# Two chains of memory segments rebuilt: output sums of all heads in three column groups of PSUM, padded memory keys, sums of exponentials redone backward

## The chip, the cores and the metric

The kernel runs on one core of a Trainium2 chip. The metric is the device time of one execution in microseconds (us), lower is better. A quoted time is the median of several executions; repeats of one kernel lie within about 0.3%. On one core a run counts as slow only if it is more than 1.5% above the fastest of the same kernel.

Engines in the profile lines: PE is TensorE's matmuls, PEld its weight loads, DVE VectorE, ACT ScalarE, POOL GpSimd, SP SyncE.

## The reference, cut to what matters

The program computes a gated mix of a plain attention A and a recurrent memory attention B, forward and with all gradients. Only B matters here. Its 2048 tokens are 64 segments of 32; each segment carries 8 rows of memory of width 576, and 32 heads of width 128 attend over memory and tokens together:

```python
for s in range(n_seg):                       # 64 segments, one after another
    h = concat([mem, x[s*32:(s+1)*32]])      # 8 + 32 rows of 576
    q, k, v = h @ Wq, h @ Wk, h @ Wv         # 32 heads of 128
    p = softmax(where(mask, q @ k.T * 128**-0.5, -1e9))   # memory keys are seen by all rows
    o = (p @ v) @ Wo
    mem = o[:8]                              # the next segment needs this
    outs.append(o[8:])
```

The kernel computes the memory rows of all segments first (the forward chain), then all token rows at once (the token attention), then the gradient of the memory from the last segment to the first (the backward chain), then the token gradients, the memory rows in token order, and the weight gradients. The two chains are serial: a segment can't start before the one ahead of it has given its memory or its gradient.

## The kernel before: the parts that matter

The forward chain, one segment, cut:

```python
for wi, w in enumerate("qkv"):               # 8 memory rows times a weight, four column groups of 512
    ... 40 matmuls into two banks of 32 x 512 blocks, evacuation to qkv
    for g in range(4):
        nc.gpsimd.dma_start(self.MT[w][...], qkv[32 * g:32 * g + MEM])   # rows for later stages
    ... 8 transposes, compacted: mE[:, wi, :] holds head by head 8 columns
for r in range(2):                           # memory keys: 16 heads against 16 heads, mask keeps the diagonal
    self.mm(S[:, 256 + r * P:...], lhsT=mE[:, 1, cs], rhs=mE[:, 0, cs], ...)
nc.scalar.activation(ET[:, :], S[:, :], ACT.Exp, scale=SCALEB)
... transposes of memory values, copy to vc, sums, value matmuls
nc.vector.reciprocal(rl[:, :, 0], po[:, 2, 0:2])
nc.gpsimd.dma_start(self.RL_m[s]..., rl[:, :, 0])            # reciprocals kept for backward
for ri in range(8):                          # output projection: head g of each four in column group g
    for lo, hi in ((0, 512), (512, D)):
        for g in range(4):
            self.mm(pw[32 * g:32 * g + 32, lo:hi], lhsT=oT[:, c0:c0 + 32], rhs=WoN[:, h, lo:hi], ..., tp=(0, 32 * g))
nc.vector.tensor_copy(ws[:, 0:320], pw[:, 0:320])            # fp32
nc.scalar.copy(ws[:, 320:D], pw[:, 320:D])
for kt in range(NKT):                        # fp32 matmuls add the four groups and turn rows to columns
    self.mm(pm[:, kt, :], lhsT=ws[:, kt * P:(kt + 1) * P], rhs=self.selF[:, :])
nc.vector.tensor_copy(mT[:, :, (s + 1) * MEM:(s + 2) * MEM], pm[:, :, :])
```

The backward chain has the same shape: 40 matmuls give dO from the gradient of the memory, a multiplication by the stored reciprocals follows, then transposes, dP, dS, three projections with the transposed weights (one pass each over 32 heads), and the same fp32 reduction. Exponentials, reciprocals and outputs come back from DRAM. In the token attention the rows of memory keys and values come from DRAM, four DMA loads each:

```python
def load_mt(self, sp, name, src, tt, r):
    ... # the tile t
    for g in range(4):
        self.nc.gpsimd.dma_start(t[32 * g:32 * g + 32, :], src[tt * 32:(tt + 1) * 32, ...])
```

The softmax here doesn't subtract the row's maximum and nothing guards it: scores larger than these inputs give would overflow.

Of the kernel before, what the change touches and what calls it, by code (L numbers as in the profile page):

```python
# [29 lines left out]
class Kern:  # L30
# [41 lines left out]

    def setup_consts(self, pool):
# [8 lines left out]
        nc.gpsimd.memset(self.onesB[:], 1.0)  # L82
        self.negonesB = pool.tile([P, P], BF16, name="negonesB")
# [10 lines left out]
        mc = pool.tile([P, 512], BF16, name="maskC")  # L94
        nc.gpsimd.memset(mc[:], 0.0)
        for ri in range(8):
            for g in range(4):
                c0 = ri * 32 + g * 8
                keep_block(mc[:, c0:c0 + 8], 8, 32 * g, 32 * g + 32)
        for r in range(2):  # L100
            for ig in range(16):
                c0 = 256 + r * 128 + ig * 8
                keep_block(mc[:, c0:c0 + 8], 8, 8 * ig, 8 * ig + 8)
        self.maskC = mc
# [26 lines left out]
        sel = pool.tile([P, MEM], F32, name="selF")  # L131
        nc.gpsimd.memset(sel[:], 0.0)
        for g in range(4):
            nc.gpsimd.affine_select(out=sel[:], in_=sel[:], compare_op=ALU.not_equal, fill=1.0, base=-32 * g,
                                    pattern=[[-1, MEM]], channel_multiplier=1)
        self.selF = sel
# [7 lines left out]
    def setup_dram(self, dram):  # L144
        T, NSEG, NM, NTT = self.T, self.NSEG, self.NM, self.NTT
        DT = lambda shape, name, dt=BF16: dram.tile(shape, dt, name=name)
        self.xT_dram = DT([NKT, P, T], "xT_dram")
        self.a_dram = DT([T, D], "a_dram")
        self.db_dram = DT([T, D], "db_dram")

        self.XT = {w: DT([T, J], f"xt_{w}") for w in "qkv"}
        self.XE = {w: DT([NTT, P, J], f"xe_{w}") for w in "qkv"}

        self.MT = {w: DT([NM, J], f"mt_{w}") for w in "qkv"}

        self.XS = {w: DT([NSEG, P, 1024], f"xs_{w}") for w in "kv"}
        self.ME = DT([NSEG, P, 3, 256], "me")
        self.ET_m = DT([NSEG, P, 512], "et_m")
        self.OT_m = DT([NSEG, P, 256], "ot_m")
        self.RL_m = DT([NSEG, 2, P], "rl_m", F32)  # L160
        self.OX = DT([T, J], "ox")
        self.OM = DT([NM, J], "om")

    def load_B_fwd(self, pool):
        nc = self.nc
        self.Wq4 = pool.tile([P, 4, J], BF16, name="Wq4")
        self.Wk4 = pool.tile([P, 4, J], BF16, name="Wk4")
        self.Wv4 = pool.tile([P, 4, J], BF16, name="Wv4")
        self.Wqk5 = pool.tile([P, J], BF16, name="Wqk5")
        self.Wv5 = pool.tile([64, J], BF16, name="Wv5")  # L170
        for W4, Wd in ((self.Wq4, self.B_Wq), (self.Wk4, self.B_Wk), (self.Wv4, self.B_Wv)):
            for kt in range(4):
                nc.sync.dma_start(W4[:, kt, :], Wd[kt * P:(kt + 1) * P, :])
        nc.sync.dma_start(self.Wqk5[0:64, :], self.B_Wq[512:576, :])
        nc.sync.dma_start(self.Wqk5[64:128, :], self.B_Wk[512:576, :])
        nc.sync.dma_start(self.Wv5[0:64, :], self.B_Wv[512:576, :])
# [8 lines left out]
    def w_nat(self, w, kt):  # L185

        if kt < 4:
            return {'q': self.Wq4, 'k': self.Wk4, 'v': self.Wv4}[w][:, kt, :], slice(0, 128)
        if w == 'q':
            return self.Wqk5[0:64, :], slice(0, 64)  # L190
        if w == 'k':
            return self.Wqk5[64:128, :], slice(64, 128)
        return self.Wv5[0:64, :], slice(0, 64)

    def b_project(self, keep, sp, psum):
# [6 lines left out]
        for tt in range(NTT):  # L202
            tok = slice(tt * P, (tt + 1) * P)
            for w in "kvq":
                tk = sp.tile([P, J], BF16, name="p_tok", bufs=2)
                te = sp.tile([P, 2, 4, 4, P], BF16, name="p_em", bufs=2)
                for c in range(8):
                    pb = psum.tile([P, 512], F32, name="p_pb", bufs=4)
                    for kt in range(NKT):
                        wap, rows = self.w_nat(w, kt)  # L210
                        self.mm(pb[:, :], lhsT=xT[rows, kt, tok], rhs=wap[:, c * 512:(c + 1) * 512],
                                start=(kt == 0), stop=(kt == NKT - 1))
# [14 lines left out]
    def b_chain_fwd(self, keep, sp, psum, WoN):  # L227
# [11 lines left out]
        self.mT = mT  # L239
        for s in range(NSEG):  # L240
            tt, sl = s // 4, s % 4
# [6 lines left out]
            mE = sp.tile([P, 3, 256], BF16, name="c_mE", bufs=2)  # L248
            S = psum.tile([P, 512], F32, name="c_S", bufs=1)
            self.mm(S[:, :], lhsT=self.identB[:, :], rhs=self.maskC[:, :], start=True, stop=False)  # L250
            for wi, w in enumerate("qkv"):
                qkv = sp.tile([P, 2, 512], BF16, name="c_qkv", bufs=4)
                for r in range(2):
                    pb = psum.tile([P, 512], F32, name="c_pb", bufs=2)
                    for kt in range(NKT):
                        wap, rows = self.w_nat(w, kt)
                        for g in range(4):
                            c = 4 * r + g
                            self.mm(pb[32 * g:32 * g + 32, :], lhsT=mT[rows, kt, s * MEM:s * MEM + 32],
                                    rhs=wap[:, c * 512:(c + 1) * 512], start=(kt == 0), stop=(kt == NKT - 1),  # L260
                                    tp=(rows.start, 32 * g))
                    self.evac(qkv[:, r, :], pb[:, :])
                for g in range(4):
                    nc.gpsimd.dma_start(self.MT[w][s * MEM:(s + 1) * MEM, :].rearrange("t (r g n) -> g t r n", r=2, g=4)[g],
                                        qkv[32 * g:32 * g + MEM, :, :])
                pt = psum.tile([P, 8, 4, 32], BF16, name="c_tr", bufs=1)
                for ri in range(8):
                    self.tr(pt[:, ri].rearrange("p g m -> p (g m)"), qkv[:, ri // 4, (ri % 4) * E:(ri % 4 + 1) * E], P)
                self.evac(mE[:, wi, :].rearrange("p (a g m) -> p a g m", a=8, g=4), pt[:, :, :, 0:MEM])
            nc.gpsimd.dma_start(self.ME[s], mE[:, :, :])  # L270
            for ri in range(8):
                self.mm(S[:, ri * 32:ri * 32 + 32], lhsT=kx[:, ri, :], rhs=mE[:, 0, ri * 32:ri * 32 + 32],
                        start=False, stop=False)
            for r in range(2):
                cs = slice(r * P, (r + 1) * P)
                self.mm(S[:, 256 + r * P:256 + (r + 1) * P], lhsT=mE[:, 1, cs], rhs=mE[:, 0, cs], start=False, stop=(r == 1))
            ET = sp.tile([P, 512], BF16, name="c_ET", bufs=2)
            nc.scalar.activation(ET[:, :], S[:, :], ACT.Exp, scale=SCALEB)
            nc.gpsimd.dma_start(self.ET_m[s], ET[:, :])
            pv = psum.tile([P, 2, P], BF16, name="c_tr", bufs=1)  # L280
            for r in range(2):
                self.tr(pv[:, r, :], mE[:, 2, r * P:(r + 1) * P], P)
            vc = sp.tile([P, 2, P], BF16, name="c_vc", bufs=2)
            self.evac(vc[:], pv[:], use="v")
            po = psum.tile([P, 3, P], F32, name="c_o", bufs=1)
            for r in range(2):
                xs, ms = slice(r * P, (r + 1) * P), slice(256 + r * P, 256 + (r + 1) * P)
                self.mm(po[:, 2, r:r + 1], lhsT=ET[:, xs], rhs=self.onesB[:, :], start=True, stop=False)
                self.mm(po[:, 2, r:r + 1], lhsT=ET[:, ms], rhs=self.onesB[:, :], start=False, stop=True)
            for r in range(2):  # L290
                self.mm(po[:, r, :], lhsT=ET[:, 256 + r * P:256 + (r + 1) * P], rhs=vc[:, r, :], start=True, stop=False)
                for i in range(4):
                    c0 = r * P + i * 32
                    self.mm(po[32 * i:32 * i + 32, r, :], lhsT=ET[:, c0:c0 + 32], rhs=vx[:, r, i * E:(i + 1) * E],
                            start=False, stop=True, tp=(0, 32 * i))
# [4 lines left out]
            with nc.allow_non_contiguous_dma(reason="column of reciprocals"):  # L300
                nc.gpsimd.dma_start(self.RL_m[s].rearrange("r p -> p r"), rl[:, :, 0])
            for i in range(4):
                nc.gpsimd.dma_start(
                    self.OM[s * MEM:(s + 1) * MEM, :].rearrange("m (r g i e) -> i g m r e", r=2, g=4, i=4)[i],
                    oc[32 * i:32 * i + 32, :, :])
            pt = psum.tile([P, 2, P], BF16, name="c_tr", bufs=1)
            for r in range(2):
                self.tr(pt[:, r, :], oc[:, r, :], P)
            oT = sp.tile([P, 280], BF16, name="c_oT", bufs=2)
            nc.gpsimd.memset(oT[:, 256:280], 0.0)  # L310
            nc.vector.tensor_copy(oT[:, 0:256], pt[:].rearrange("p r n -> p (r n)"))
            nc.gpsimd.dma_start(self.OT_m[s], oT[:, 0:256])
            if s == NSEG - 1:
                break
            pw = psum.tile([P, 640], F32, name="c_pw", bufs=1)
            for ri in range(8):
                for lo, hi in ((0, 512), (512, D)):
                    for g in range(4):
                        h = (ri // 4) * 16 + g * 4 + ri % 4
                        c0 = ri * 32 + g * MEM  # L320
                        self.mm(pw[32 * g:32 * g + 32, lo:hi], lhsT=oT[:, c0:c0 + 32], rhs=WoN[:, h, lo:hi],
                                start=(ri == 0), stop=(ri == 7), tp=(0, 32 * g))
            ws = sp.tile([P, 640], F32, name="c_ws", bufs=1)
            nc.vector.tensor_copy(ws[:, 0:320], pw[:, 0:320])
            nc.scalar.copy(ws[:, 320:D], pw[:, 320:D])
# [1082 lines left out]
```

## Time and profile before

11818.32 us median of four runs (11794.58 to 11826.19); the profiled execution spans 11807.0 us. I cut the run at the first and last starts of each stage's tiles; clock is the mean that the throttle granted TensorE in the stage, 1.00 being full speed.

| stage | us | clock |
|---|---|---|
| attention A, projections, weights | 5937 | |
| forward chain | 1420 | 0.81 |
| token attention | 1511 | 0.77 |
| backward chain | 1151 | 0.88 |
| token gradients | 983 | 0.74 |
| memory rows | 118 | 0.51 |
| weight gradients | 687 | |

How to read it: a chain's stage is 63 spacings between segments plus a start, so the spacing of the copies that write the memory is its best measure (22.14 us forward, 17.07 backward, means). The lines of the stages, of a forward segment and of the waits are in the prediction (in the timeline: start, length, engine, line, what, count, in brackets the idle time before it).

### The profile page before, as it was taken

Reading aid. Unit: us, or ns where it says so; the run is one execution under the profiler, and the core shown is the slowest. Engines: PE = TensorE matmul, PEld = TensorE weight load, DVE = VectorE, ACT = ScalarE, POOL = GpSimd, SP = SyncE. Lnnn points to the kernel's source line nnn. Section 1 sums busy time; section 2 is a strip of 40 time slices with the busy share of each in tenths; the row PEclk is TensorE's granted clock in tenths of the full one; section 3 lists DMA queues with packets and bytes.
Section 4 is the critical chain, followed back from the end, with each engine's and each line's share of the span. In section 5 each row is a group of like instructions: output and inputs, shape, how many; then the busy total and the mean of one; then the engine's idle time right before and its main releaser. Section 6 shows DMA issues by size and latency. Waiting matters only on the chain. (4 is left out here: it accounts for less than half of the span.)

```text
span 11807.0 us, 189310 instructions
## 1 busy us (share of the span) xinstructions
PE 10704.6 (91%) x79411; PEld 4101.3 (35%) x79798; DVE 4365.5 (37%) x6102; ACT 3510.0 (30%) x4681; POOL 2793.4 (24%) x5477
## 2 busy tenths in 40 slices
PE   7999999999999999989888888888887888999799
PEld 2212121212121212134433333555544554555444
DVE  4555555555555555534311111333332222122200
ACT  3444444444444444423311111222221111111100
POOL 3000000000000000013245555333334444333100
PEclk8555555555555555589888877777778988777799
DMA  2000000000000000045532222555544333555544
GB/s 66 1 4 1 4 1 4 1 4 1 4 1 1 4 1 1 1 144 231 201 83 54 54 55 70 190 174 167 176 152 149 90 93 94 186 188 187 192 147 145
DMA packets 583499, 980.07 MB, mean 83 GB/s; under 512 B 213801, under 2 KB 392114, under 8 KB 564402
## 3 DMA queue, kind: packets, MB, share of 16 engines
q1 hardware_dynamic: 421506, 632.91, 16.9%
q0 software_dynamic: 159824, 333.70, 8.4%
q8 instruction: 624, 10.22, 0.4%
q14 instruction: 233, 1.91, 0.1%
q10 hardware_dynamic: 1312, 1.33, 0.0%
HBM read 542.17 MB, written 425.07 MB: 82 GB/s over the span
## 5 line engine op out<-in xcount | busy, mean ns | idle before, releaser
L1178 DVE TENSOR_TENSOR a_U<-a_w,a_E 128x1024 bf16<-128x1024 f32 x1024 | 1252.1, 1224 | 1131.5 <-ACT a_E L1176 1088.1
L1105 DVE TENSOR_TENSOR a_U<-a_w,a_E 128x1024 bf16<-128x1024 f32 x1024 | 1253.4, 1225 | 962.5 <-ACT a_E L1103 962.3
L1176 ACT ACTIVATE a_E<-a_w 128x1024 bf16<-128x1024 f32 x1024 | 1049.1, 1025 | 1375.6 <-PE a_w L66 1373.1
L1103 ACT ACTIVATE a_E<-a_w 128x1024 bf16<-128x1024 f32 x1024 | 1048.8, 1025 | 1179.5 <-PE a_w L66 1179.5
L66 PE MATMUL a_w<-a_kaug,a_qaug 19*128 19x512 bf16 x2048 | 901.7, 600 | 4.8 <-ACT a_E L1176 4.1
L66 PE MATMUL a_w<-a_vaugT,a_doaT 19*128 19x512 bf16 x2048 | 836.0, 620 | 22.0 <-DVE a_U L1178 16.1
L66 PE MATMUL a_acc<-a_E,a_dog 128*32 128x512 bf16 x2048 | 625.0, 600 | 71.8 <-ACT a_E L1176 0.2
L66 PE MATMUL a_w<-a_doT,a_vaugT 19*128 19x512 bf16 x2048 | 670.8, 623 | 5.2 <-ACT a_E L1103 4.0
L66 PE MATMUL a_w<-a_qaug,a_kaug 19*128 19x512 bf16 x2048 | 658.0, 599 | 3.6 <-ACT a_doT L63 3.0
L1137 POOL TENSOR_TENSOR a_otok<-a_tk,a_rl 128x144 bf16<-128x144 f32 x64 | 27.4, 428 | 2570.8 <-DVE a_rl L1136 2570.8
L66 PE MATMUL a_acc<-a_U,a_ku 128*32 128x512 bf16 x2048 | 625.3, 607 | 0.2
L66 PE MATMUL a_acc<-a_U,a_qtok 128*32 128x512 bf16 x2048 | 623.1, 606 | 0.6 <-DVE a_U L1178 0.6
L66 PE MATMUL w_acc<-w_col,w_h 128*128 128x512 bf16 (+1 forms) x2352 | 523.4, 381 | 13.5 <-DMA w_col<-dqx 10.8
L1081 POOL DMA_DIRECT2D a_dog<-do_dram x8 | 4.7, 589 | 1814.1 <-PE a_acc L66 1810.0
L61 DVE CAST p_tok<-p_pb 128x512 bf16<-128x512 f32 x384 | 265.4, 692 | 318.4 <-PE p_pb L66 318.4
L66 PEld LDWEIGHTS <-a_qaug 19*128 19x128 bf16 x2048 | 152.2, 98 | 655.5 <-issue 655.5
L66 PE MATMUL a_acc<-a_E,a_evB 128*64 128x512 bf16 x1024 | 325.6, 612 | 54.0 <-ACT a_E L1103 0.6
L66 PEld LDWEIGHTS <-w_h 128*128 128x128 bf16 (+1 forms) x2400 | 237.4, 100 | 299.6 <-issue 34.3
L66 PEld LDWEIGHTS <-a_dog 128*32 128x32 bf16 x2048 | 108.9, 100 | 652.4 <-issue 652.2
L63 ACT COPY p_em<-p_tr 128x512 bf16<-128x512 bf16 x384 | 225.0, 586 | 357.8 <-PE p_tr L71 357.6
L66 PEld LDWEIGHTS <-d_g 128*32 128x32 bf16 x12288 | 271.4, 104 | 170.8 <-issue 60.7
L66 PEld LDWEIGHTS <-a_ku 128*32 128x32 bf16 x2048 | 105.9, 101 | 639.3 <-issue 639.2
(476 smaller groups left out, 16390.7 us busy)
## 6 DMA issues: line engine op xcount, KB each, us to landing
xt_k<-p_tok SPq DMA_DIRECT2D x16, 1024.0 KB
xe_k<-p_em POOLq DMA_DIRECT2D x16, 1024.0 KB
xs_k<-p_seg POOLq DMA_DIRECT2D x64, 256.0 KB
xt_v<-p_tok SPq DMA_DIRECT2D x16, 1024.0 KB
xe_v<-p_em POOLq DMA_DIRECT2D x16, 1024.0 KB
xs_v<-p_seg POOLq DMA_DIRECT2D x64, 256.0 KB
xt_q<-p_tok SPq DMA_DIRECT2D x16, 1024.0 KB
xe_q<-p_em POOLq DMA_DIRECT2D x16, 1024.0 KB
```

Source lines behind the costliest of these rows:

```text
L61: nc.vector.tensor_copy(out, in_)
L63: nc.scalar.copy(out, in_)
L66: return self.nc.tensor.matmul(out, lhsT, rhs, start=start, stop=stop, tile_position=tp, skip_group_check=True)
L1081: nc.gpsimd.dma_start(dog[:, :, :], self.do_dram[g])
L1103: nc.scalar.activation(ex[:], s[:], ACT.Exp, scale=SCALEA)
L1105: nc.vector.tensor_tensor(out=u[:], in0=d[:], in1=ex[:], op=ALU.mult)
L1137: nc.gpsimd.tensor_tensor(out=osl, in0=v[:, :, :, o0:o0 + DA], in1=rl[:].to_broadcast([P, 4, 2, DA]), op=ALU.mult)
L1176: nc.scalar.activation(ex[:], s[:], ACT.Exp, scale=SCALEA)
L1178: nc.vector.tensor_tensor(out=u[:], in0=d[:], in1=ex[:], op=ALU.mult)
```

## The change

It shortens the path of a segment. The output sums of all heads collect in PSUM itself: each head's 576 columns are cut into three groups of 192 that run side by side, and all 32 heads accumulate, so that a bf16 copy of 96 rows and seven small bf16 matmuls replace the fp32 reduction. Memory keys and values stay padded, which saves the transposes of the values. The sums of exponentials over memory keys, and their reciprocals, are no longer stored but redone in the backward chain; rows that went to DRAM in token order are made by transposes where they are needed, or in the stage of the memory rows. "Filler" matmuls on a spare bank are to hold the clock through short waits. The diff, cut to its core:

```diff
+    def busy(self, pf, n, rhs):
+        w = rhs.shape[-1]
+        for _ in range(n):
+            self.mm(pf[0:32, 0:w], lhsT=self.identB[:, 0:32], rhs=rhs)
 # forward chain
-                for g in range(4):
-                    nc.gpsimd.dma_start(self.MT[w]..., qkv[32 * g:32 * g + MEM, :, :])
+            self.busy(pf, 2, mE[:, 0:512])            # after the scores
+            self.busy(pf, 4, ET[:, :])                # after the value matmuls
+            self.busy(pf, 4, oc[...])                 # after the transposes of the output
-                for lo, hi in ((0, 512), (512, D)):
-                    for g in range(4):
-                        self.mm(pw[32 * g:32 * g + 32, lo:hi], lhsT=oT[...], rhs=WoN[:, h, lo:hi], ...)
+                for g in range(4):
+                    for j in range(3):
+                        self.mm(pw[32 * j:32 * j + 32, :], lhsT=mEw(3, c0, c0 + 32), rhs=Wo[:, h, 192 * j:192 * j + 192],
+                                start=(ri + g == 0), stop=(ri + g == 10), tp=(0, 32 * j))
 # ... cut ...
+    def rows_to_columns(self, sp, psum, pre, pw, dst, late):
+        nc.scalar.copy(ws[0:96, 128:192], pw[0:96, 128:192])
+        nc.vector.tensor_copy(ws[0:96, 0:128], pw[0:96, 0:128])
+        self.busy(self.pf, 2, late)
+        for kt, p0, j, c0, n in (...):                # 3 matmuls that need the first copy, 4 that need the second
+            self.mm(pt[p0:p0 + n, kt, :], lhsT=ws[0:96, c0:c0 + n], rhs=self.identB[0:96, 32 * j:32 * j + 32], tp=(0, p0))
+        self.busy(self.pf, 1, late)
+        nc.vector.tensor_copy(dst, pt[:, :, 0:MEM])
 # backward chain
+            self.mm(S[:, :], lhsT=self.identB[:, :], rhs=self.maskD[...], start=True, stop=False)   # scores redone
+            ...
+            nc.scalar.activation(ET[:, 256:512], S[:, :], ACT.Exp, scale=SCALEB)
+            for x in range(2):
+                self.mm(Sg[:, 1, :], lhsT=self.onesPB[:, :], rhs=ET[:, 256 * x:256 * x + 256], ...)
+            nc.vector.reciprocal(rlb[:, :], Sg[:, 1, :])
-                nc.vector.tensor_tensor(out=dO[:, r], in0=pb[:], in1=rl[:, r].to_broadcast([P, 4, E]), op=ALU.mult)
+                self.evac(dO[:, r], pb[:, :], use="vs"[r])
+            self.busy(self.pf, 2, dO[:, 0])
+            self.busy(self.pf, 1, dO[:, 1])
 # ... 8 transposes of dO, product with rlb ...
+            self.busy(self.pf, 3, dO[:, 1])
+            self.busy(self.pf, 2, dOc[...])           # after dP
 # token attention (token gradients alike)
-                mv = self.load_mt(sp, "x_mv", self.MT["v"], tt, r)
+                mv = self.tok_me(sp, psum, "x_mv", me, 1)          # four transposes and a copy
 # the token gradients load the transposed weights again, after the backward chain
```

The count per backward segment: eleven fillers (3 and 3 of 512 columns around dO, 2 of 256 after dP, 3 of 512 in the reduction).

## The prediction

> **What bounds the kernel now.** The page's two lines of busy shares say that TensorE is busy nearly everywhere, but the granted clock differs from slice to slice, so I cut the run into stages (ends read from first and last starts of each stage's tiles) and asked for the table of stretches. Columns: stretch, its length in us, busy time and count of PE, weight loads, DVE, ACT, POOL, then granted TensorE clock, DMA share, GB/s.
>
> ```profile
> 5937.00:7361.00 1424.00, 1233.97 (x15740) 535.73 (x15741) 279.86 (x670) 217.23 (x479) 771.21 (x1340) 0.81 0.24 60
> 7361.00:8905.00 1544.00, 1273.87 (x11181) 761.56 (x11305) 507.02 (x1045) 431.12 (x772) 571.68 (x925) 0.77 0.53 177
> 8905.00:10022.00 1117.00, 954.54 (x18817) 566.86 (x18817) 279.09 (x672) 119.49 (x288) 516.17 (x1007) 0.89 0.33 96
> 10022.00:11002.00 980.00, 948.71 (x7101) 503.00 (x7199) 189.75 (x447) 161.87 (x288) 325.18 (x734) 0.74 0.58 184
> 11002.00:11115.00 113.00, 58.73 (x433) 45.00 (x432) 45.23 (x154) 30.04 (x57) 43.15 (x112) 0.52 0.90 279
> ```
>
> In order: forward chain, token attention, backward chain, token gradients, memory rows. The change leaves the first 5937 us and the last 692 us (weight gradients) as they are. The chains, 2541 us together, are 64 segments one after another: each needs the memory that the one before made. So no engine's share bounds them; the latency of one segment does. From the starts of the copy that writes a segment's memory I took the spacing: forward mean 22.13 us (20.2 to 24.1), backward mean 17.06 us (mostly 16.7 and 17.4 in turn).
>
> The timeline shows where a forward segment's time lies; these are the lines between its scores and the next segment (start, length, engine, line, what; in brackets idle time before it).
>
> ```profile
> 6617.79 0.60 ACT L278 ACTIVATE c_ET<-c_S 128x512 bf16<-128x512 f32 x1
> ...
> 6619.08 0.29 DVE L61 COPY c_vc<-c_tr 128x256 bf16<-128x256 bf16 x1 [0.51 <-PE c_tr L71]
> ...
> 6621.27 0.29 DVE L311 COPY c_oT<-c_tr 128x256 bf16<-128x256 bf16 x1 [0.45 <-PE c_tr L71]
> ...
> 6621.62 2.14 PE L66 MATMUL c_pw<-WoN,c_oT 128*32 128x512 bf16 x64 [0.45 <-DVE c_oT L311]
> ...
> 6623.89 0.49 DVE L324 COPY c_ws<-c_pw 128x320 f32<-128x320 f32 x1 [2.32 <-PE c_pw L66]
> 6624.41 0.37 ACT L325 COPY c_ws<-c_pw 128x256 f32<-128x256 f32 x1 [6.03 <-DVE c_ws L324]
> ...
> 6624.43 1.28 PE L66 MATMUL c_o<-selF,c_ws 128*128 128x8 f32 x10 [0.67 <-DVE c_ws L324]
> ...
> 6625.75 0.20 DVE L330 CAST c_mT<-c_o 128x40 bf16<-128x40 f32 x1 [1.37 <-PE c_o L66]
> 6626.01 1.05 PE L66 MATMUL c_pb<-Wq,c_mT 128*32 128x512 bf16 x16 [0.29 <-DVE c_mT L330]
> ...
> 6642.04 4.03 PE L66 MATMUL c_pw<-WoN,c_oT 128*32 128x512 bf16 x64 [0.45 <-DVE c_oT L311]
> ```
>
> The reader is to see two things. The reduction after the output projection (copies in fp32, DVE then ACT, ten fp32 matmuls, a copy) takes from 6623.76 to 6626.01, 2.25 us of hand-over. And the same 64 matmuls last 2.14 us in one segment and 4.03 us in the next: a segment with idle stretches pays the half clock later, on its dense matmuls. DMA is not the limit in either chain (shares 0.24 and 0.33).
>
> The waits of TensorE tell which stages have slack for added TensorE work:
>
> ```profile
> PE x_p L66 <- POOL x_pr L495: 102.8, 128, 1.7
> PE x_b L66 <- DMA g_mo<-om: 12.1, 1, 12.1
> ```
>
> The first is the longest in the token attention, the second in the token gradients, where it is a single start-up wait. So the gradients (PE busy 948.71 of 980) have no slack at all, the attention has some.
>
> **What the Trainium skill says.** "TensorE: Matmul & The Clock Gate", Part 1, has the array at half rate after idle windows of about 3.4 us and at full rate after a busy one; the 2.14 against 4.03 us agrees. Its Part 3 has matmuls in different 32-column groups run side by side; here 64 projection matmuls of 512 and 64 columns follow one another in 1.96 us (in the backward chain, from the first matmul with Wk at 9450.61 to the first with Wq at 9452.57), which is 32 x 576 columns / 4 groups / 2.4 columns per ns = 1.92 us, so it agrees. "PSUM — Partial Sum Buffer", PSUM bank collisions, wants accesses of two engines to one bank kept apart; the DVE and ACT halves of the fp32 copy above do run in turn. "TensorEngine Tiling (Array Packing)", Key Properties, says that a change of tiling mode drains the array; in the chains the 64-row matmul quads take 0.33 us and the 128-row ones 0.243 us, which fits. The change keeps those.
>
> **The change, part by part. Forward chain, one segment, at full clock.**
> - Projections q, k, v stay: six blocks of 0.97 + 0.33 = 1.30 us, with some twenty transposes between (four take 0.33 us): 7.8 + 1.65 = 9.45; the warm part of the trace runs slightly slower, so 9.7. Before, q ran at half clock in most segments (2.38 us a block, not 1.30).
> - From the last v matmul to the output projection: 6617.04 to 6621.62 = 4.6 us before. Memory values are now used from the padded rows, so the transposes and copy to c_vc (about 0.8 us between the end of the exponential and the first matmul that uses c_vc) go. New: 16 small score matmuls at about 0.026 us spacing (0.42, before 0.5), exponential 0.6, sums and 16 value matmuls 0.75, reciprocal 0.17, scaling 0.42, transposes 0.28, copy 0.29, eight hand-overs of about 0.07: 3.75 us. Filler matmuls (2, 4 and 4 of 512, 512 and 256 columns: 0.43, 0.85, 0.43 us) lie in waits of about that length.
> - Output projection: 32 heads, three groups of 192 columns side by side: 192/2.4 = 80 ns a head, 2.56 + 0.2 us latency. That uses three quarters of the groups: 0.6 us slower than 2.14, but far below 4.03.
> - Reduction: ACT copy of 64 columns 0.22, DVE 128 columns 0.28, in turn; seven bf16 matmuls 0.3; copy 0.2; hand-overs 0.3: 1.35 us for 2.25.
> - Sum: 9.7 + 3.75 + 2.75 + 1.35 = 17.5 us against 22.13. Times 63: **-290 us**. POOL's DMA issues (4 x 3 rows of q, k, v, four of om and others, over 10 us a segment) go as well; beside the path today, but they would not have fitted well in 17 us.
>
> **Backward chain, one segment.** dO matmuls 2.6 (same). Copy, transposes, product with the reciprocals (now on the transposed side, 0.42 for 0.29), dP: about 3.0 (2.74 before). From dP to the projection 1.1 (2.4 before), because dS is halved and v's heads start as soon as their gradient is there. Projection 96 heads x 82 ns = 7.85, with transposes and the q, k gradients between, 0.45, latency 0.15: 8.45 (6.7 before, partly at half clock). Reduction 1.35 (2.26). Redone scores, exponential, sums: 0.8 us of PE for segment s-1, mostly in waits, 0.2 on the path. Sum 16.7 against 17.06: **-23 us** over 63. What the reduction gives, the three-group projection takes. The weights come first for dO (4.7 MB, then 13.8 MB), so the first segment starts some 12 us sooner: **-12**.
>
> **What is paid elsewhere.**
> - Token gradients: a second load of the transposed weights, 13.8 MB, at the 420 GB/s that the stretch 8895 to 8915 shows is 33 us; a third may load early, and 12 us of start-up wait are there today: +22. Rows now made by transposes, 8 a half-tile at 0.08 to 0.15, and 16 matmuls with minus ones, 0.25 to 0.4: 1.15 us x 32 = +37, on a TensorE with no slack.
> - Token attention: the same 8 transposes, 0.65 to 1.2 us x 32 = 30, but with waits to hide in: +10.
> - Memory rows: 16 blocks for 12 at about 7 us: +28.
> Together **+97 us**.
>
> Total: -290 - 23 - 12 + 97 = -228; 11819.84 - 228 = about 11592, and I add 8 us for start-up of the new pools: 11600.
>
> **Rivals.** (1) The fillers do not hold the clock: dense matmuls then stay at 0.81 to 0.9 as now; about 1.5 us a forward segment and 0.7 a backward one come back (estimate: the excess of 4.03 over 2.14, and q's, in half the segments), total about 11730. For it: the clock follows activity in windows of some 3.4 us (same section), and fillers are only 0.2 to 0.85 us. Against it: they fill just the waits listed above. (2) Three groups of 192 run slower than 80 ns a head, because three weight loads a head are not hidden: at 100 ns the backward chain loses 1.9 us a segment, the forward 0.6: about 11755. Against it: weight loads of four groups start together in the trace. (3) A fixed instruction order makes the redone sums or fillers stall TensorE: +0.5 us a segment is +63 us. (4) The chain falls further, to 16.5 and 16, because more of the redone work and the fillers hide than I count: about 11480. (5) Memory traffic bounds a chain: shares of 0.24 and 0.33 speak against it.
>
> **Range and chances.** The gain I derive, 220 us, is 1.9%; the line of 2% lies at 11583, inside the uncertainty of the chains (some 40 us each) and of the costs elsewhere (25). So faster or same is nearly a coin toss, with a slight lean to same since sums of latencies leave things out; slower would need rivals 1 to 3 together. Range 11470 to 11720.
>
> **What would show it.** Spacing of the copies that write the memory: 17.5 forward, 16.7 backward. Granted clock near 1.0 in both chains. Output projection of 32 heads in about 2.75 us, in every segment alike; no fp32 matmul. Token gradients about 1040 us, memory rows about 140. Wrong if the clock stays under 0.9, if a head takes well over 80 ns, or if TensorE waits on a recomputed sum in the backward chain.

## More of the kernel before

In the timeline of the kernel before (start, length, engine, line, what, count, in brackets the idle time before it) the 40 dO matmuls stand in one piece of 2.68 us, the transposes of dS begin 6.13 us after the first of them:

```profile
9440.22 2.68 PE L66 MATMUL d_pb<-WoTb,d_gT 128*32 128x512 bf16 x40 [0.28 <-DVE d_gT L725]
...
9446.35 0.37 PE L71 MATMUL d_tr<-identB,d_dS 128*128 128x128 bf16 x2 [0.67 <-DVE d_dS L684]
```

## The result, and the profile after

The changed kernel takes 11708.77 us median of four runs (11695.72 to 11713.39), beside 11818.32 us before: the ratio is 0.9909, 95% interval 0.9892 to 0.9926. Ratios here and below are the mean time of one kernel's fast runs over that of the other's in the same rounds, so they aren't quite the ratio of the medians. The gain is 110 us where 220 were predicted; the range (11470 to 11720) held the time and the direction was right.

The same stretches of the changed kernel (stretch, length, busy time and count of PE, PEld, DVE, ACT, POOL, then clock, DMA share, GB/s):

```profile
5931.60:7089.10 1157.50, 1145.35 (x19023) 577.34 (x19023) 265.30 (x637) 225.23 (x447) 33.41 (x128) 0.99 0.18 54
7089.10:8641.00 1551.90, 1355.82 (x11571) 795.77 (x11570) 520.73 (x1078) 447.84 (x802) 432.75 (x772) 0.75 0.48 160
8641.00:9867.20 1226.20, 1158.46 (x25800) 806.39 (x25801) 336.01 (x673) 173.70 (x418) 8.48 (x65) 0.97 0.28 91
9867.20:10877.60 1010.40, 963.22 (x7968) 520.28 (x7967) 161.08 (x352) 179.95 (x320) 166.14 (x480) 0.77 0.62 192
10877.60:11024.80 147.20, 75.39 (x558) 58.34 (x558) 62.89 (x202) 39.42 (x73) 56.45 (x148) 0.51 0.92 285
```

Both chains now run at a clock near full, and yet the backward chain is longer than before. Stage by stage, against the prediction:

| stage | before | after | change | predicted |
|---|---|---|---|---|
| up to the forward chain | 5937 | 5932 | -5 | 0 |
| forward chain | 1420 | 1158 | -262 | -290 |
| token attention | 1511 | 1552 | +41 | +10 |
| backward chain | 1151 | 1226 | **+75** | -35 |
| token gradients | 983 | 1010 | +27 | +59 |
| memory rows | 118 | 147 | +29 | +28 |
| start of new pools | | | | +8 |
| sum (profiled runs) | | | -95 | -220 |

The forward chain did nearly what was wanted. Its segments are 17.9 us apart, every one alike. In the timeline of the changed kernel these lines answer to those of the prediction, from the exponential to the next segment's first matmul:

```profile
6513.52 0.60 ACT L292 ACTIVATE c_ET<-c_S 128x512 bf16<-128x512 f32 x1
...
6516.43 2.82 PE L66 MATMUL c_S<-Wo,c_mE 128*32 128x192 bf16 x96
...
6519.29 0.21 ACT L332 CAST c_ws<-c_S 96x64 bf16<-96x64 f32 x1 [4.75 <-PE c_S L66]
6519.53 0.29 DVE L333 CAST c_ws<-c_S 96x128 bf16<-96x128 f32 x1 [3.16 <-ACT c_ws L332]
...
6519.77 0.39 PE L66 MATMUL c_pf<-c_mE,identB 128*32 128x512 bf16 x1
6520.09 0.47 PE L66 MATMUL c_tr<-identB,c_ws 96*128 96x32 bf16 x4
...
6520.85 1.05 PE L66 MATMUL c_pb<-Wq,c_mT 128*32 128x512 bf16 x16
```

The projection takes 2.82 us for 96 matmuls, at full clock, in every segment but the first; the reduction takes 6520.85 - 6519.29 = 1.56 us. DVE's copy ends at 6519.82, but the four matmuls that need it start at 6520.09: the filler of 6519.77 stands in front of them.

In the backward chain (spacing 18.28 us, all between 18.0 and 18.8) the same happens on a larger scale:

```profile
9428.44 0.60 PE L66 MATMUL d_pb<-WoTb,d_gT 128*32 128x512 bf16 x5
9428.46 0.38 ACT L653 ACTIVATE d_ET<-d_g 128x256 bf16<-128x256 f32 x1 [1.37 <-DVE d_gT L340]
9428.98 0.39 PE L66 MATMUL d_g<-d_ET,onesPB 128*128 128x256 bf16 x2
...
9429.52 0.83 PE L66 MATMUL d_pb<-WoTb,d_gT 128*32 128x512 bf16 x11
...
9432.29 0.81 PE L66 MATMUL d_pf<-d_dO,identB 128*32 128x512 bf16 x3 [0.31 <-DVE d_dO L61]
9433.03 0.62 PE L71 MATMUL d_tr<-identB,d_dO 128*128 128x128 bf16 x8
9433.58 0.82 PE L66 MATMUL d_pf<-d_dO,identB 128*32 128x512 bf16 x3
...
9435.80 0.28 PE L71 MATMUL d_tr<-identB,d_dS 128*128 128x128 bf16 x2
```

The redone sums stand after the fifth dO matmul and wait there for an exponential, so the 40 matmuls are in pieces. Three fillers read the copy of dO, so they can't start until the wait that they were to fill is over, and the transposes of dO, which want the same copy, come after them. The prediction had named this as a sign that it would be wrong: TensorE waits here on a recomputed sum. From the first dO matmul to the transposes of dS it is now 7.36 us, where it was 6.13.

### The profile page after: what moved, and what is told of

It reads as the page before. It is cut to its first block, busy times and chain, and to the rows that moved or that the text cites. A ratio compares the mean times of both kernels' runs of the same rounds, so it can differ in the third digit from the quotient of the medians.

```text
span 11711.6 us, 208963 instructions
## 1 busy us (share of the span) xinstructions
PE 10959.3 (94%) x91222; PEld 4451.6 (38%) x91222; DVE 4411.1 (38%) x6054; ACT 3615.3 (31%) x4858; POOL 1254.4 (11%) x2894
## 5 line engine op out<-in xcount | busy, mean ns | idle before, releaser
L66 PEld LDWEIGHTS <-d_g 128*32 128x32 bf16 x18432 | 498.8, 97 | 30.1 <-issue 11.1
L66 PEld LDWEIGHTS <-a_qtok 128*32 128x32 bf16 x2048 | 107.8, 101 | 623.8 <-issue 623.4
L66 PE MATMUL a_acc<-a_E,a_evA 128*64 128x512 bf16 x1024 | 325.2, 633 | 0.0
```

The source lines that it names most:

```text
L66: return self.nc.tensor.matmul(out, lhsT, rhs, start=start, stop=stop, tile_position=tp, skip_group_check=True)
```

## The experiments

Twelve kernels ran. All but one are correct; the exception is said. Some expectations speak of the compiled order of TensorE's instructions; I read the order from the timelines.

| run | change to the changed kernel | median us | ratio to before [95%] |
|---|---|---|---|
| changed kernel | none | 11708.77 | 0.9909 [0.9892, 0.9926] |
| e1_bwd_nofill | no fillers backward | 11632.06 | 0.9845 [0.9831, 0.9860] |
| e2_fwd_nofill | no fillers forward | 11699.18 | 0.9904 [0.9887, 0.9920] |
| e3_recip_stored | reciprocals stored and loaded | 11952.99 | 1.0120 [1.0105, 1.0136] |
| e4_prep_early | redone work moved earlier | 11728.35 | 0.9930 [0.9915, 0.9945] |
| e5_wt_once | transposed weights loaded once | 11675.01 | 0.9882 [0.9867, 0.9897] |
| e6_red_nofill | no fillers in the backward reduction | 11639.39 | 0.9853 [0.9838, 0.9867] |
| e7_fill_const | backward fillers read a constant | 11663.74 | 0.9876 [0.9861, 0.9890] |
| e8_att_rows | token attention without transposes (wrong) | 11679.69 | 0.9884 [0.9868, 0.9901] |
| e9_fill_waits | three backward fillers of eleven | 11614.73 | 0.9834 [0.9814, 0.9854] |
| e10_fwd_red_nofill | no fillers in the forward reduction | 11700.38 | 0.9904 [0.9887, 0.9921] |
| e11_best | e5, e9 and e10 together | 11580.73 | 0.9803 [0.9786, 0.9820] |
| e12_before_tr | kernel before, with the transposes in its token attention | 11856.6 | 1.0039 [1.0015, 1.0063] |

### Do the fillers cost the backward chain? (e1)

My first theory (A in what follows) was that the fillers stand in the path. Its rivals: that they are needed to hold the clock, and (B) that the redone sums and their reciprocal set the segment.

```diff
-        for _ in range(n):
+        for _ in range(n if self.fill else 0):       # fill is off in the backward chain
```

> The changed kernel without the filler matmuls of the backward chain alone. Theory A (fillers stand in TensorE's fixed order ahead of work that is ready: three of 512 columns ahead of the dO transposes, one ahead of the second part of the memory transposes): the spacing of backward segments falls from 18.28 to 17.5 to 17.8 us, the stage by 30 to 50 us, clock stays at 0.95 or more. Rival (fillers are what holds the clock at 0.97): the clock in this stage falls to about 0.9, as before the change, and the spacing stays at 18.2 or rises to 19. Other stages unchanged.

Measured: the stage falls from 1226 to 1148 us, more than theory A expected, its clock from 0.97 to 0.95. The spacing is 16.7 us in most segments, which is the figure of the prediction, and 17.9 us or more in 14 of 63 (mean 17.05). In the timeline of this kernel the dO matmuls are whole again and the redone sums lie ahead of them, in the reduction's waits:

```profile
9402.64 0.38 PE L66 MATMUL d_g<-d_ET,onesPB 128*128 128x256 bf16 x2
...
9403.12 1.76 DVE L659 RECIPROCAL d_rlb<-d_g 128x256 f32<-128x256 f32 x1
9403.17 1.05 PE L66 MATMUL d_pb<-WoTb,d_gT 128*32 128x512 bf16 x16
...
9409.13 0.29 PE L71 MATMUL d_tr<-identB,d_dS 128*128 128x128 bf16 x2 [0.41 <-DVE d_dS L728]
...
9409.46 0.84 PE L66 MATMUL d_pw<-WTcv,d_g 128*32 128x192 bf16 x24
```

Set side by side, the two timelines give the account of one segment. First dO matmul to the last group of dO matmuls: 9428.44 to 9431.58 with fillers, 9403.17 to 9405.45 without, +0.86 us. From there to the transposes of dS: 4.22 against 3.68, +0.54. From ACT's copy in the reduction to the copy that writes the gradient: 1.30 against 1.09, +0.21. From that copy to the next dO matmul: 0.26 against 0.34, -0.08. All other pieces agree (9.27 us from the transposes of dS to ACT's copy in both). The sum is 1.53 of the 18.28 - 16.7 = 1.58 us. The largest piece, 0.86, isn't a filler at all but redone work that the fillers in the reduction had pushed out of its place.

What the clock takes back shows in a slow segment of the same run. The 24 matmuls that take 0.84 us above take 1.47:

```profile
8776.49 0.39 PE L71 MATMUL d_tr<-identB,d_dS 128*128 128x128 bf16 x2 [0.41 <-DVE d_dS L728]
8776.92 1.47 PE L66 MATMUL d_pw<-WTcv,d_g 128*32 128x192 bf16 x24
```

Full speed is back by 8780.33. The clock that the throttle granted is in the trace too, so this needn't be guessed from durations. Below are two stretches: this one in e1, and the whole backward chain of the changed kernel after its first 65 us.

```profile
8776.50:8779.80 3.30, 3.30 (x53) 2.52 (x53) 1.02 (x3) 0.37 (x1) 0.00 (x0) 0.50 0.56 179
8706.40:9867.20 1160.80, 1141.75 (x25669) 798.56 (x25661) 330.69 (x664) 170.81 (x412) 7.76 (x62) 1.00 0.25 77
```

After the start of the stage, the clock record of e1 has 14 stretches at 0.50, each 3.41 us long: one in each of the 14 slow segments and none in another. With the fillers there is none. So the rival has something in it, about 14 x 1.3 = 18 us, against some 100 us that the fillers cost.

### And forward? (e2)

```diff
-        for _ in range(n):
+        for _ in range(n if self.fill else 0):       # fill is off in the forward chain
```

> The changed kernel without the filler matmuls of the forward chain alone. If the fillers hold the clock there: clock falls from 0.99 towards 0.81 to 0.9, spacing of forward segments rises from 17.94 to 19 or more, uneven. If the clock would hold anyway: spacing 17.6 to 17.8 (the reduction loses the 0.27 us that one filler stands in front of the memory transposes), clock 0.97 or more.

Measured: stage 1150 for 1158 us, clock 0.97 for 0.99, the whole 11699 us: no difference that the intervals resolve. The segments are 17.5 us, exactly the prediction's figure, with 19.1 in every fourth or fifth. In these 14, and in no others, the clock record has one stretch of 3.41 us at 0.50, and the projection of 96 matmuls runs at half clock for most of its length:

```profile
6510.64 4.47 PE L66 MATMUL c_S<-Wo,c_mE 128*32 128x192 bf16 x96 [0.38 <-DVE c_mE L315]
```

Forward, the fillers pay what they cost, 0.4 us a segment against 1.6 in every fourth or fifth. The clock's rise from 0.81 to 0.97 came without them; I take the shorter waits for its cause, which no run shows by itself.

### Is it the redone sums and their reciprocal? (e3, e4)

Rival B: the reciprocal of 128 x 256 sums takes 1.76 us on DVE, which the prediction hadn't costed, and delays the copy of dO. In e3 the forward chain stores its reciprocals and the backward chain loads them; sums and reciprocal are gone.

```diff
+                nc.gpsimd.dma_start(self.RL_m[s].rearrange("(r p) -> p r", r=2), rl[:, :, 0])    # forward
-            for x in range(2): self.mm(Sg[:, 1, :], lhsT=self.onesPB[:, :], ...)                 # backward
-            nc.vector.reciprocal(rlb[:, :], Sg[:, 1, :])
+            nc.sync.dma_start(rlb[:, :], self.RL_m[s].partition_broadcast(P))
```

> The redone sums undone: the forward chain stores its 256 reciprocals a segment, the backward chain loads them to all partitions; scores and exponentials are still redone. Theory B (the 1.76 us reciprocal on DVE delays the copy of dO, and the two matmuls of column sums wait for the exponential inside the dO matmuls): backward spacing falls from 18.28 to 17.3 to 17.7 us, stage by 40 to 60 us. Rival (the delay is TensorE's order and fillers, the reciprocal only fills DVE's idle time): falls by less than 0.3 us.

Measured: the backward spacing stays at 18.21 us (stage 1221): with the fillers in place, sums and reciprocal don't set it, and B fell. The exponentials are still redone, and their transposes still stand after the fifth dO matmul, so e3 clears the sums and the reciprocal alone. The forward chain got worse for the store alone, from an even 17.9 us to 17.9 to 28.3 (mean 21.4, stage 1376), which makes the whole 1.2% slower than before. The kernel before has a store of the same kind in its forward chain. Its waits there are spread over all engines; what makes them I didn't settle.

In e4 the redone work of segment s-1 is issued in segment s, after the projection of v's gradient.

```diff
             project(3, "v", 16, 32)
+            if s > 0:
+                ready = prepare(s - 1)       # scores, exponential, sums, reciprocal, transposes
             project(2, "k")
```

> Same work, other order: loads, scores, exponential, sums, reciprocal and transposes of segment s-1 are issued in segment s after v's projection instead of at the start of segment s-1. Theory B: all of the redone work but TensorE's 0.8 us leaves the path; spacing 17.0 to 17.5 us, stage 50 to 80 us shorter. Rival (TensorE is simply full, busy 0.94 of the stage): the work only changes place, spacing 18.0 or more.

Measured: 18.52 us, stage 1242, a little worse: the work costs in the projections about what it costs among the dO matmuls. Of the three places seen (among the dO matmuls, in the projections, in the reduction's waits as in e1) the last is the cheapest. Whether it is free there isn't shown: no run leaves the redone work out with the fillers gone.

### Place or amount? (e6, e7, e9)

e6 takes only the three fillers of the backward reduction away.

```diff
-            self.rows_to_columns(sp, psum, "d", pw, gT[...], g4[:, 256:768])
+            self.rows_to_columns(sp, psum, "d", pw, gT[...], None)       # None: no fillers
```

> Only the three fillers of the reduction are off in the backward chain; the eight others (3 and 3 of 512, 2 of 256 columns) stay. In the compiled order of TensorE the redone sums and transposes then lie between the reduction's own matmuls, and the 40 dO matmuls are unbroken, where in the changed kernel they stand after the fifth dO matmul. Theory A1 (most of the loss is redone work pushed into the dO matmuls: 3.47 us for 2.6, and 0.27 us of filler in the reduction): segment 18.28 falls to about 17.1, stage 1226 to about 1152. Theory A2 (most of the loss is the fillers after dO and after its transposes, each 0.2 to 0.3 us in front of waiting transposes): segment stays at 17.8 or more, stage above 1195.

Measured: spacing 17.27 us, stage 1162. Three fillers of eleven make 64 of the 78 us that all eleven make: theory A1 holds. In the timeline the redone sums go back into the reduction as soon as those three are gone. The account of e1 had 0.86 + 0.21 = 1.07 us for these two pieces, and 18.28 - 17.27 = 1.01 was measured. The piece from the last dO matmuls to the transposes of dS is 4.06 us here (9399.68 to 9403.74), against 3.68 without fillers: 0.38 us is what the eight fillers left cost there.

e7 keeps all eleven but lets them read a constant tile, so that none waits for a copy.

```diff
-            self.busy(self.pf, 2, dO[:, 0])
-            self.busy(self.pf, 1, dO[:, 1])
+            self.busy(self.pf, 3, fc)              # fc: a constant 128 x 512 mask; the others alike
```

> All eleven fillers of the backward chain stay, with the same widths, but read a constant tile, so that none waits for the copy that ends the wait it should fill; the compiler then places them within the waits and the redone work lies in the reduction. Theory A (place, not amount): segment about 16.8 to 17.0, all alike, clock 0.97 or more, stage 1135 to 1150, the whole 11620 to 11635. Rival (amount: 11 fillers of 0.1 to 0.3 us cannot fit in this segment): segment 17.8 or more, stage above 1195.

A miss for both theories: stage 1189 us, between them. With nothing to wait for, the fillers were placed ahead of their turn: 349 of them ran before 8739 us, and none was left after 9321. So one run holds both cases. In the 33 segments before 9321 us the redone work lies in the reduction and there are about eleven fillers a segment: 17.75 us mean (17.55 to 18.45), and none holds a stretch at half clock. In the other 29 there are none: 16.7 us in many, 18.0 in some, mean 17.18, and six of the slow ones hold a stretch at half clock. Where they run, three of them last longer than the wait that e1 shows at that place (0.58 us in front of the transposes of d_g):

```profile
9001.81 0.82 PE L66 MATMUL d_pf<-maskX,identB 128*32 128x512 bf16 x3
9002.56 0.28 PE L71 MATMUL d_tr<-identB,d_g 128*128 128x128 bf16 x2
```

So amount matters too: eleven fillers cost about 1 us a segment against the 16.7 us of segments at full clock, even where nothing is displaced.

e9 keeps three: one of 512 columns after the transposes of dO, two of 256 after dP.

```diff
-            self.busy(self.pf, 2, dO[:, 0])
-            self.busy(self.pf, 1, dO[:, 1])
-            self.busy(self.pf, 3, dO[:, 1])       # after the transposes of dO
+            self.busy(self.pf, 1, dO[:, 1])
             self.busy(self.pf, 2, dOc[...])       # after dP: stays
-            self.rows_to_columns(sp, psum, "d", pw, gT[...], g4[:, 256:768])
+            self.rows_to_columns(sp, psum, "d", pw, gT[...], None)
```

> Backward chain with three of its eleven fillers: one of 512 columns after the transposes of dO and two of 256 after the copy of dO's columns; none after the dO matmuls and none in the reduction. In the compiled order the redone work lies in the reduction, as without fillers. Theory A (fillers cost where they stand in front of waiting work, and pay where TensorE waits 0.6 us anyway): segments 16.7 to 16.9, nearly all alike instead of every third or fourth at 18.0, stage about 1135, the whole about 11620. Rival (the half-clock stretches of the filler-free chain come whatever these three do): stage 1148 to 1160, segments of 18.0 still there every third or fourth.

Measured: 11614.73 us, stage 1133, spacing 16.81 us, longest 17.6; the segments of 18.0 are gone, and so are the stretches at half clock after the first 65 us. This is the first version whose backward chain clearly beats that of the kernel before (1151; e1 came to 1148).

```profile
8637.10:9770.20 1133.10, 1032.34 (x25289) 766.67 (x25289) 336.08 (x673) 173.68 (x418) 8.48 (x65) 0.97 0.31 98
```

TensorE is busy 126 us less than with eleven fillers (1158.46 above) at the same clock of 0.97.

### The reload of the weights (e5)

In the changed kernel TensorE waits 43.2 us at the start of the token gradients, for the queue that now carries the transposed weights a second time; this line answers to the 12.1 us of before:

```profile
PE x_b L66 <- DMA g_dqe<-dqe: 43.2, 1, 43.2
```

e5 keeps the weights in SBUF from the backward chain on.

```diff
+            with SB("p4w") as p4w:
+                k.alloc_WT(p4w)
                 with SB("p4o") as p4o, SB("p4s") as p4s, PS("p4p") as p4p:
                     k.b_chain_bwd(bk, p4o, p4s, p4p)      # loads them, keeps them
-                k.load_WT(p4w)
```

> The transposed weights that the backward chain has in SBUF stay for the token gradients; the second load of 13.8 MB goes. Nothing else changes. Theory (the reload is on the path: TensorE's first x_b matmul of the token gradients waits 43.2 us for DMA in the changed kernel, 12.1 us before): the stage falls from 1010 us to about 979, the whole to about 11678 (-31 us). Rival (a wait that is hidden behind the start of the stage's own tile loads, which now share the queue with it): the stage falls by less than 10 us.

Measured: the stage falls to 976 us, 34 less, and the wait is gone. That is also 7 us below the kernel before (983), so the +37 that the prediction put on transposes and extra matmuls doesn't show in the time:

```profile
9860.60:10836.50 975.90, 961.54 (x7968) 519.49 (x7967) 161.38 (x353) 180.19 (x320) 166.44 (x480) 0.78 0.60 185
```

PE's busy time there rose by 13 us (948.71 to 961.54), while the granted clock rose from 0.74 to 0.78. Length times clock estimates the work at full speed: 983 x 0.74 = 727 us before and 976 x 0.78 = 761 in e5, 34 more. By this estimate the +37 was right as work, and the higher clock paid for it; what raised the clock no run shows.

### The token attention (e8, e12)

The stage grew by 41 us where 10 were predicted. The transposes are the only new work on TensorE. But in the changed kernel the tiles of 128 tokens don't take a little more each: of 15 spacings 12 are about 95.5 us and 3 are about 92.2 (the expectation of e12 below counts 13 and 2); before, all 15 are 92.2 (92.1 to 92.3). 12 x 3.3 = 40 us is the whole growth. Laid over each other, a long tile and a short one differ in stretches where the same matmuls run at half speed. First from a long tile, then from a short one of the same run:

```profile
7348.20 0.63 PE L71 MATMUL x_tr<-identB,x_dst 128*128 128x128 bf16 x4
7350.77 0.59 PE L71 MATMUL x_tr<-identB,x_dsm 128*128 128x128 bf16 x4 [0.16 <-ACT x_sq L63]
...
7725.97 0.39 PE L71 MATMUL x_tr<-identB,x_dst 128*128 128x128 bf16 x4
7728.09 0.38 PE L71 MATMUL x_tr<-identB,x_dsm 128*128 128x128 bf16 x4 [0.16 <-ACT x_sq L63]
```

e8 loads the rows of memory keys and values in place of the transposes (from token rows of the same shape, so the result is wrong).

```diff
-                mk = self.tok_me(sp, psum, "x_mk", me, 0)
+                mk = self.rows_me(sp, "x_mk", "k", tt, r)     # one DMA; mv alike
```

> Wrong result on purpose in outputs that depend on the token attention: its rows of memory keys and values are loaded by DMA from token rows (same shape and bytes) in place of eight transposes and two copies a half-tile. Theory (the transposes are the whole of the stage's growth, 1.2 us a half x 32): the stage falls from 1552 us back to about 1512, as before the change. Rival (the growth comes from elsewhere in the stage, such as the loads and re-orderings of the padded memory): it stays above 1540.

Measured: 1535 us, between the two theories. Tiles of both lengths again, now the other way round: about 5 of 15 are long. e12 is the counter-test, the kernel before with the transposes:

```diff
-                mk = self.load_mt(sp, "x_mk", self.MT["k"], tt, r)
+                mk = self.tok_me(sp, psum, "x_mk", me, 1)
```

> The kernel before with one part of the change alone: in the token attention the rows of memory keys and values come from eight transposes a half-tile in place of eight DMA loads; all else as before. In the kernel before every tile takes 92.2 us; in the changed kernel 13 of 15 take about 95.5 and 2 take 92.2, with the same matmuls at 0.63 us in place of 0.38 for stretches of some 3 us. Theory C (the eight transposes by themselves are hidden, but shift the waits so that each tile holds one or two more half-clock stretches): most tiles go to about 95.5, the stage from 1511 to about 1550, its clock from 0.77 to 0.75. Rival D (the transposes cost 1.2 us a half directly): every tile 94 to 94.6, the clock stays at 0.77. Rival E (the growth comes with the rest of the change, such as the stage before or the loads of the padded memory): tiles stay at 92.2, stage about 1511.

Measured: 13 of 15 tiles at 95.4 to 95.8, two at 92.0 and 92.5, the stage at 1561 us:

```profile
7366.70:8927.80 1561.10, 1328.88 (x11435) 800.24 (x11564) 521.86 (x1078) 447.27 (x802) 433.73 (x653) 0.74 0.49 162
```

Theory C holds. The transposes alone are enough to turn the tiles long; by themselves they are hidden, since a tile that holds them can still take 92.2 us; what costs is more time at half clock. Over the two tiles of the changed kernel shown above the granted clock is 0.71 (7286.03 to 7381.71, long) and 0.81 (7665.11 to 7757.27, short). e8 says that they aren't the only thing in the changed kernel that can do so. What tips a single tile I don't know.

### The rest of the fillers, and the best of all (e10, e11)

e10 takes the three fillers of the forward reduction away.

```diff
-            self.rows_to_columns(sp, psum, "c", pw, mT[...], mE[:, 512:1024])
+            self.rows_to_columns(sp, psum, "c", pw, mT[...], None)
```

> Forward chain without the three fillers of the reduction; the ten others stay; backward chain as in the changed kernel. Theory A: they stand in front of the memory transposes for about 0.3 us, as in the backward chain, so a segment goes from 17.9 to 17.6 and the stage from 1158 to about 1139, all segments alike, clock 0.99. Rival (forward, the ten others or the clock set the 17.9): stage 1150 or more, or segments of 19.1 come back as in the run without any forward filler.

Measured: 17.7 us, every segment alike, clock 0.99, stage 1144 us. That is 13 us less than with them, where theory A expected 19: right in kind, two thirds in size. In the whole (11700.38 us) it doesn't rise above the spread of the runs.

e11 puts the edits of e5, e9 and e10 together, shown above.

> All that helped together: weights kept (-33 us), backward chain with three fillers (about -90 us), forward chain without reduction fillers (about -19 us). If the three are independent, as they are in different stages, the whole is 11709 - 142 = about 11567; forward 1139, backward 1135, token gradients 976 us. Rival (the clock's budget or the state of the token attention moves with them): above 11600.

Measured: 11580.73 us, ratio 0.9803 to the kernel before, which beats both kernels: by 2.0% (interval 1.8 to 2.1%) and, from the two ratios (0.9803 / 0.9909), by 1.1%. Its stages are 1145, 1555, 1137 and 976 us. It lands 14 us above the expectation: 6 of them in the forward stage, 2 in the backward one, 3 in the token attention, where the expectation had taken the changed kernel's 1552; the rest is within the spread of the runs.

## Why the prediction was right in direction and short in size

**Forward chain: right, with luck in one part.** The step to 17.5 us a segment held to its four parts: v's matmuls end 9.78 us after the start (9.7), the projection starts 3.74 later (3.75), takes 2.86 until ACT's copy (2.75). The reduction is 1.56 for 1.35, and 0.2 of that is its fillers (e10). Without any filler a segment is 17.5. The luck is in the 3.75: the pieces that the prediction lists for it add up to 3.49, and a wait that it read as about 0.8 us is 1.04 in the timeline (6618.39 to 6619.43). One forward spacing before was 18.7 us, below its "20.2 to 24.1". A head costs 2.64 us / 32 = 82.5 ns in the backward projections, so rival 2 fell from the first trace.

**Backward chain: the step that failed.** The words were: "Redone scores, exponential, sums: 0.8 us of PE for segment s-1, mostly in waits, 0.2 on the path", and of the forward fillers "lie in waits of about that length". The term was 0.2 us; it measured 1.6 a segment more, 18.28 for 16.7. By the account of e1, 0.9 of it is redone work displaced from the reduction into the dO matmuls, 0.2 the reduction's own fillers (these two together 64 us in e6), and 0.5 lies between the dO matmuls and dS, of which e6 leaves 0.4 to the fillers there, late or longer than their waits (e1, e7). The sum of the other terms was right: without fillers the segment is 16.7. Rival 3, a fixed order that makes redone sums or fillers stall TensorE, is what came; it was put at +0.5 us a segment and was three times that. The gain of 12 us from an earlier first segment didn't come either: stage less 63 spacings is 76 us before and 74 after.

**Fillers and the clock.** Rival 1 said that the fillers wouldn't hold it. They do (0.99 and 0.97), but most of the rise is there without them (0.97 and 0.95). What is missing to 1.00 with fillers is the start of each stage. The prediction took the fillers as free and the clock as their merit; both were off. Length times clock (an estimate, since waits don't stretch with the clock) shows how much the clock did: forward 1420 x 0.81 = 1150 us before and 1158 x 0.99 = 1146 after, backward 1151 x 0.88 = 1013 before, 1226 x 0.97 = 1189 after and 1148 x 0.95 = 1091 in e1. So by this estimate nearly all of the forward gain is clock and not less work, and the backward chain got longer at equal clock even without fillers, as the projection of 8.45 us for 6.7 in the prediction lets expect.

**Token attention: wrong by 31 us.** "With waits to hide in" was right of the transposes themselves, which in a short tile cost nothing; the +10 missed that they turn most tiles to more time at half clock (e12).

**Token gradients: 32 us too dear.** The reload cost 31 to 34 (22 said). For the +37 for transposes and matmuls "on a TensorE with no slack" the stage shows 7 us less than before, since the clock rose with them (e5). The step that read busy 948.71 of 980 as "no slack" took busy time at 0.74 of the clock for full use.

**Memory rows:** +29 for +28.

Together: +28 forward, +110 backward, +31 attention, -32 gradients, +1 rows and -13 at the start make 125 us between the -220 predicted and the -95 of the profiled runs.

## What to carry to other kernels

Work put into a wait is free only if it can start when the wait starts and ends before it does: a filler that reads the very copy that everyone waits for stands in front of the work, and three small matmuls in TensorE's order can move others that had a good place. So add them one place at a time, look at the order, and read the spacing of segments. And a busy share at a reduced clock isn't a full engine: ask which clock a stage runs at before calling it full or slack.

## What the Trainium skill lacked or had wrong

- "TensorE: Matmul & The Clock Gate", Part 1, has the half rate come after an idle window of about 3.4 us and warns of gaps of that length; its section on PSUM-queue cycling speaks of micro-idles, without sizes. Here half-clock stretches come where the longest wait of TensorE in the segments read is 0.74 us: in every fourth or fifth forward segment of e2 (waits of 0.33, 0.74 and 0.38 us ahead of the projection) and in 14 of 63 backward segments of e1 (0.26, 0.58 and 0.41). The length of a stretch agrees with the page: 3.41 us in the clock record of both runs. Each costs 1.3 to 1.6 us. Nor does the page say that a stage with many short waits can take either of two lengths, 92.2 or 95.5 us a tile in one run of one kernel.
- "VectorE: DVE Perf Modes", First, the fixed hardware budget, says that Reciprocal is an iterative divide with a repeat count of 8, and gives no time. Here it takes 1.76 us for 128 x 256 fp32 values, where a product of that many takes 0.42; for 128 x 2 it takes 0.17.
- No page says what filler matmuls are worth. Here three a backward segment (one of 512, two of 256 columns) removed the segments of 18.0 us (e9), eleven cost 1.6 us a segment in the changed kernel and 1.05 in e7, both against the 16.7 us of a segment at full clock without any, and thirteen forward came out even (e2).
